# Four products of the first unit in half contractions, two of them in the k^T v banks, and a new set of ranks for the front

## Chip, cores and metric

The kernel runs on one core of one Trainium2 chip. The metric is the device time of one execution in microseconds (us), from runs of the whole kernel; lower is better.

## What is computed

Linear attention with 8 batches of 8 heads, 576 positions and 64 channels a head, then a mixture of 8 experts over the 4608 tokens, weighted by a Sinkhorn-balanced routing matrix:

```python
phi = lambda x: np.where(x > 0, x, np.exp(x) - 1.0) + 1.0
q_p, k_p = phi(q), phi(k)
kv  = einsum('bhsd,bhse->bhde', k_p, v);  z = k_p.sum(axis=2)
x   = einsum('bhsd,bhde->bhse', q_p, kv) / (einsum('bhsd,bhd->bhs', q_p, z)[..., None] + 1e-06)
# x becomes (4608, 512): tokens by 8 heads x 64
P = np.exp(logits - logits.max())            # logits = x @ w_gate, (4608, 8)
for _ in range(8):
    P /= P.sum(1, keepdims=True) + 1e-09
    P /= P.sum(0, keepdims=True) + 1e-09
    P *= N / E
out = sum over e of P[:, e:e+1] * (np.maximum(x @ w1[e], 0) @ w2[e])   # w1: 512x1024, w2: 1024x512
```

## The kernel before

**A planner writes the order.** The kernel doesn't issue its work in the order of the source. Every step is added to a plan (`_Plan.add`) with the engine or engines it may run on, a cost, the steps it depends on, the buffers that it takes, and a priority. `_Plan.run` then plays the plan: whenever an engine is free, the step that can start first is taken, among those ready the one with the lowest priority number, and its instructions are emitted. Each engine then runs its instructions in exactly that order on the chip. The costs, the added latencies (`lat`) and the release times (`after`) are numbers in the source; they decide the order, and nothing else. At the end of the source a string of ranks gives some 240 steps another priority, and in part a fixed engine: `92:3.7509:dve` sets step 92's priority to 3.7509 and puts it on DVE. Steps are counted in the order in which they are added.

**The attention front.** `att(b, g)` is one of 16 attention steps, counted n = 2b + g; each handles four heads of one batch. Its loads `kin`, `qin`, `vin` (L253, 576 KB each) have two buffers per name, so the load of step n waits until step n - 2 has used its own. SP issues them, except those of n = 2 and 3, which POOL issues between the loads of w1 and w2 of expert 0 (L207, two halves each, converted to 16 bits on the way). Then come, by name of the tile:

- `ek`, `eq`: exp on ACT (L266), then the minimum with 1 on DVE (L275)
- `tk`, `tq`: the feature map. Either ACT adds 1 (L272) and DVE takes the maximum (L278), or DVE does both in two pieces (L281)
- `vv`: v as 16 bit (L221 on ACT, L223 on DVE)
- `kv_ps`: k^T v on PE (L309), 18 matmuls, in the PSUM banks `ye2` and `ye3`; its copies `kvz`, four small ones, on ACT or DVE
- `qt_ps`: nine transposes of tq (L335), copied to `qpT` in two pieces
- `den_ps` (L350), `rden` with its reciprocal (L356, L358), `num_ps` (L374), `xn` in three pieces (L379, DVE)
- `xt_ps`: transposes of xn (L390), copied to the shared `xT` (L221, L223), which holds x transposed for the whole kernel

`logits` (L408) and the routing iterations follow when the batches they need are there. Ahead of the first real matmul, and between the early ones, PE runs 47 warm-up matmuls, `yw` (L481), of lowest priority.

**Expert 0.** `unit_plain(0, g)` for nine groups g of 512 tokens does the two plain layers: `layer1` makes eight products `hq` of 128 x 512 (L546, four matmuls each, one for each quarter c of the contraction over 512 channels), each followed by a ReLU on ACT (`h`, L550); then the second layer makes four products `ye` of eight matmuls (L736), cut in two halves of four: the first needs only the first half of w2, the second the other. The results are copied to `acc` (ACT L221 or DVE L223). The planner puts these products between the attention steps; unit 0 is g = 0.

**PSUM.** There are eight banks: `ye0` to `ye3`, two of `hq` (pool `hqp`), two of `att` (pool `aps`, which qt, den, num, xt and logits share). A product of unit 0 needs a bank of its own until its ReLU has read it.

**Half contractions.** The quarters c = 0, 1 of `xT` come from attention step n = 0, the quarters c = 2, 3 from n = 1. In unit 0 the first two products are cut in two jobs, the first of which needs only n = 0:

```python
jobs = [(f, 0, NDT) for f in range(NFT)]
if g == 0:
    jobs = [(f, c, c + 2) for c in (0, 2) for f in range(2)] + jobs[2:]
```

**Experts 1 to 7** (`block7`, L640, and `unit`, L843) use products with combined operands that save one of eight. They need `x_blocks`, which stores combinations of `xT` in `xd` by SP, to be loaded again as `xs` (L598). The order of their PE work is written out by hand in `order`, and the ranks of this change don't reach it.

Of the kernel before, what the change touches and what calls it, by code (L numbers as in the profile page):

```python
# [10 lines left out]
FP32 = mybir.dt.float32  # L11
# [111 lines left out]
def kernel(  # L123
# [17 lines left out]
    P = 128  # L141
# [4 lines left out]
    NFT = F // P  # L146
# [4 lines left out]
    S_ = _Plan()  # L151
# [5 lines left out]
    yps = ctx.enter_context(tc.tile_pool(name="yps", bufs=1, space=PSUM))  # L157
    hqp = ctx.enter_context(tc.tile_pool(name="hqp", bufs=2, space=PSUM))
# [26 lines left out]
    p_att, p_hq, p_h = S_.pool(2), S_.pool(2), S_.pool(2)  # L185
# [4 lines left out]
    p_ye = [S_.pool(1) for _ in range(4)]  # L190
# [41 lines left out]
    def fadd(*a, **kw):  # L232
        t = add(*a, **kw)
        front_ids.append(t)
        return t

    def att(b, g):
        n = 2 * b + g
        pr = n - 100.0
# [7 lines left out]
        gin, tin, gt, tph = {}, {}, {}, {}  # L247
        for nm, ten in (("k", k), ("q", q), ("v", v)):
            gr = gin[nm] = S_.grp(p_in[nm])

            def fn(_, gr=gr, nm=nm, ten=ten):
                gr["tile"] = fp.tile([P, 2, NJ, D], FP32, tag=nm + "in", name=nm + "in", bufs=2)
                (nc.gpsimd if n in (2, 3) else nc.sync).dma_start(  # L253
                    out=gr["tile"].rearrange("p r j d -> p r (j d)"),
                    in_=AP(tensor=ten.tensor, offset=(b * H + 4 * g) * S * D, ap=src))
            ti = fadd(("pool", 1.0) if n in (2, 3) else ("sp", 0.45), fn, acq=[gr], prio=pr,
                      deps=[w_last[0] if n in (2, 3, 4) else None, in_prev[0]])
            in_prev[0] = ti
            tin[nm] = fadd(("dma", 1.55), lambda _: None, deps=[ti], use=[gr], prio=pr, lat=2.6)
        for nm in "kq":  # L260
            ge = S_.grp(p_e)
            gt[nm] = S_.grp(p_t[nm])
# [30 lines left out]
        def f_v(e):  # L293
            copy(e, gvv["tile"][:, :, :, 0:D], gin["v"]["tile"])
        tvv.append(fadd(("act", 1.17) if n < 2 else ("dve", 0.75), f_v, deps=[ta, tin["v"]],
                        use=[gvv, gin["v"]], prio=pr))
# [32 lines left out]
        for j0, j1 in ((0, 5), (5, NJ)):  # L329
# [8 lines left out]
            def f_qc(e, j0=j0, j1=j1, gp=gp):  # L338
# [3 lines left out]
                           use=[gp, gq], prio=pr))  # L342
# [147 lines left out]
    for i in range(2):  # L490
        nc.vector.memset(vv_t[i][:, :, :, D], 1.0)
        nc.vector.memset(kvz_t[i], 0.0)
    att(0, 0)
    att(0, 1)
    w_t = {0: load_w1(0, prio=-290.0, parts=2, deps=[gates[0]])}
    for b in range(1, B):
        att(b, 0)
        att(b, 1)
        if b == 1:
            w_t[0] += load_w2(0, prio=-96.5, parts=2, deps=[in_prev[0]])  # L500
        if b % 2 == 1:
            logits(b // 2)
# [22 lines left out]
    def layer1(e, g):  # L525
        gw1, tw1, gw2, tw2 = w_t[e]
        bs = range(512 * g // S, (512 * g + 511) // S + 1)
        xd_ = [xt_done[(b, c)] for b in bs for c in range(NDT)]
        th = []
        gh = S_.grp(p_h)  # L530

        def f_ha(_):
            gh["tile"] = hpool.tile([P, NFT, 512], FP16, tag="h", name="h")
        tha = add(("none", 0.0), f_ha, deps=[prev_hq[0]], acq=[gh], prio=g - 400.0)
        ghqs = [S_.grp(p_hq) for f in range(NFT)]
        jobs = [(f, 0, NDT) for f in range(NFT)]
        if g == 0:
            jobs = [(f, c, c + 2) for c in (0, 2) for f in range(2)] + jobs[2:]
        for f, c0, c1 in jobs:
            ghq = ghqs[f]  # L540

            def f_hq(_, f=f, ghq=ghq, c0=c0, c1=c1):
                if c0 == 0:
                    ghq["tile"] = hqp.tile([P, 512], FP32, tag="hq", name="hq")
                for c in range(c0, c1):
                    nc.tensor.matmul(ghq["tile"], lhsT=gw1["tile"][:, c, ts(f, P)], rhs=xT[:, c, ds(512 * g, 512)],  # L546
                                     start=(c == 0), stop=(c == NDT - 1))

            def f_rl(_, f=f, ghq=ghq):
                nc.scalar.activation(out=gh["tile"][:, f, :], in_=ghq["tile"], func=AF.Relu)  # L550
            t1 = add(("pe", 0.2175 * (c1 - c0)), f_hq, deps=[tw1[f // 4], prev_hq[0]] + xd_[0:c1 if g == 0 else None],
                     acq=[ghq] if c0 == 0 else [], use=[gw1] + ([ghq] if c0 > 0 else []),
                     prio=g + 0.1 * f + 0.35)
            prev_hq[0] = t1
            x_users.append(t1)
            if c1 < NDT:
                continue
            th.append(add(("act", 0.6), f_rl, deps=[t1, tha], use=[ghq, gh], prio=g - 400.0))
        return gh, [th, th]
# [369 lines left out]
    for tt in (3, 2, 1, 0):  # L929
# [2 lines left out]
            chain.append(pe_id[f"z{tt}{half}"])  # L932

    ranks = """
        43:-88.9997 46:-94.9994:act 55:-94.9991:dve 56:-94.9985:dve 66:4.15 68:-94.9985 71:-89.0006
        74:-392.9979:dve 85:-89.0003:dve 92:3.7509:dve 96:-97.9985 99:-94.9991:dve 107:-392.9967
        110:-95.0006:act 133:-94.9991 139:-95 146:4.1497 152:-88.9994 153:-94.9994:dve 154:-94.9997
        166:-95.0003:act 172:-398.0018:dve 173:4.1497:dve 174:-97.9988:dve 199:-398.0021 200:-94.9988
        209:-88.9991 216:-94.9973 226:-94.9991 235:-94.9997 246:-90.9976:dve 248:-94.9997 255:-95.0003:act
        256:-90.9973:act 257:-397.9985:act 261:-94.9997 263:-95.0003 265:-397.9994 267:-392.9982 269:-398  # L940
        284:-95.0003:dve 286:-95 288:-398.0024 290:-95.0009 294:-392.9976:act 296:-95.0042:dve 298:-95.0003
        299:-98:dve 300:-94.9991 305:-95.0006 307:-95.0003 309:-397.9988 310:-392.9997 311:-393.0006 321:-95
        323:-95.0006 324:-88.9994 326:-95 328:-88.9997 331:-90.9982 334:-392.9985:act 338:-94.9991 340:-94.9997
        343:-97.9997 349:-89.9994 350:-95.0015:dve 353:8.3497 362:-97.9997:act 366:-88.9985 370:-95.0006
        376:-94.9994 377:-90.9985:dve 378:-88.9988 379:-90.0012:act 383:-95.0006 385:-90.9985 387:-88.9991
        392:-90.0018:dve 403:-94.9979:act 406:-95.0009 408:-88.9988 411:-85.0009:dve 414:-89.0009 416:-88.9991
        418:-88.9994 421:-90.0018 423:-395.0012 427:-95.0018 429:-90.0018 444:-88.9997 446:-88.9985
        447:-97.9991:act 448:-90.9997:act 454:-85.0009 459:-89.0012 461:-90.9988 463:-90.9982 467:-95.0018
        476:-90.0012:dve 482:-90.0015 486:-94.9973:act 487:-90.0009:act 488:-89:act 490:-89.9997
        491:-95.0015:act 492:-95.0009 493:-90.0012:dve 494:-395 499:-85.0015 501:-90.9985 505:-99.003  # L950
        516:-95.0012:act 526:-89.0003:act 532:-395.0015 533:-94.9988 534:-90.9985 535:-395.0021 540:-90.9979
        543:-394.9994 545:-395.0006 554:-90.0012 563:-395.0012 565:-395.0012:dve 569:-90.9982 571:-85.0015
        573:-89.9997 576:-96.0006 578:-96 580:-90.9979 585:8.3482:dve 593:-90.9976:act 595:-85.0006
        601:-395.0024 607:-89.0021 609:-90.9985 616:3.75 618:-95.0042 630:-89.0003 640:-88.9988 646:-96.0009
        647:-395.0015:dve 648:-395.0012 650:-395.0009 653:-395.0018 655:-97.9994 659:3.7515 666:8.3485
        671:-90.9985 678:8.7491 684:8.6479 717:-99.003 723:-95.0009 725:-94.9994:dve 731:-398.0021:act
        733:3.7509 735:-98 742:-94.9994 744:-94.9991 749:-95.0003 754:-94.9994 756:-94.9991 759:-398.0003
        762:-95.0003 763:-95.0003 764:-97.9997 768:-90.0012:act 769:8.3491 774:8.6485 776:8.6488 791:-94.9976
        793:-90.0009 796:-90.0015 797:-90.9985 799:-89.0006 800:4.1515 801:-88.9991 803:-95.0006 804:-95.0003
        806:-89.9988 809:-90.0012:act 816:3.7512 818:-395.0006 824:-90.9988 826:-90.0018 830:-395 836:-90.0012  # L960
        838:-395.0009 839:-90.9985 840:-89.0009 844:-395.0018 845:-89.0006 850:-94.9982:act 854:-94.9979:act
        856:-395.0006 865:-88.9994 866:-90.0009 867:-90.9979 868:-88.9997 875:-395.0024 897:8.3494 898:3.75
        906:-85.0009 910:8.6509 916:-89 918:3.7494 920:-85.0012 924:3.7509 926:-395.0033 928:3.7497 929:-90.9994
        931:8.6512 938:-96.0015 947:1.7518 957:-395.0015 959:-96.0027 961:-96.0006 964:8.3488 969:8.3494
        979:3.7518 988:-90.9988 990:-90 992:8.3491 998:-395.0021 1000:3.7512 1006:3.7479 1009:8.7488 1010:8.7482
        1016:3.7512:act 1017:8.6518 1020:8.7503 1031:8.7494 1039:-85.0012 1041:-94.9997 1043:-90.9994
        1049:3.7518 1051:-95.0012 1052:8.6491 1060:8.3479 1061:8.6482
    """
    for w in ranks.split():
        n, p, *en = w.split(":")  # L970
# [35 lines left out]
```

## Time and profile before

| | us |
|---|---|
| median of 6 runs | 977.54 |
| the six runs | 975.72, 975.76, 975.84, 979.25, 979.57, 980.36 |
| profiled execution | 975.4 |
| its span | 973.6 |

| engine | busy us | share of the span |
|---|---|---|
| PE | 963.9 | 99% |
| DVE | 767.6 | 79% |
| ACT | 569.1 | 58% |
| POOL | 111.7 | 11% |

The span is the time from the first to the last instruction in the trace; the profiled execution's own time is 1.8 us longer. The share of PE counts a matmul as busy until its modelled end. The shares of DVE and ACT are means over stages that differ: the attention front takes the first 138 us, in which ACT is busy over 90% of most slices from 40 to 120 us. The granted TensorE clock is full throughout.

Where the loads of the start land, by issue and landing time (us): k, q, v of n = 0 at 5.1, 6.5, 8.1; of n = 1 at 9.6, 11.0, 12.5; w1's halves, issued at 8.2 and 9.0, at 15.2 and 17.75; k, q, v of n = 2 at 19.3, 21.2, 22.7; of n = 3 at 24.1, 25.6, 27.0; w2's halves, issued at 17.8 and 18.6, at 30.6 and 36.3; k, q, v of n = 4, issued by SP at 24.7, 26.5, 27.2, at 31.7, 35.1, 36.9.

### The profile page before, as it was taken

What the parts mean: (1) busy time and instruction counts of PE and PEld (TensorE: products, weight loads), DVE (VectorE), ACT (ScalarE), POOL (GpSimd) and SP (SyncE); (2) the same over time, 40 slices, a digit from 0 to 9 for tenths busy, and PEclk for the clock granted to TensorE, in tenths of its full rate; (3) what the DMA queues carried; (4) which work ended last, traced back from release to release, by engine and by line L of the source; (5) the groups of instructions that cost most, each with busy time, mean ns of one, the idle gap of its engine ahead of it and who ended that gap; (6) DMA issues with size and microseconds to landing.
All of it is one profiled execution on the core that took longest, in us unless ns stands there. A gap on an engine that the chain in (4) does not pass through costs nothing.

```text
span 973.6 us, 21442 instructions
## 1 busy us (share of the span) xinstructions
PE 963.9 (99%) x8737; PEld 794.0 (82%) x8737; DVE 767.6 (79%) x1563; ACT 569.1 (58%) x1049; POOL 111.7 (11%) x158
## 2 busy tenths in 40 slices
PE   8999999999999999999999999999999999999998
PEld 4556564588888888888888888888888888888886
DVE  6899778987777778777777777777777887777775
ACT  6899945555555555555555555555555555555553
POOL 3000000111111111111111111111111111111110
PEclk9999999999999999999999999999999999999999
DMA  9987925562227222272226222272226322236664
GB/s 317 283 271 241 231 78 189 168 147 77 76 77 157 84 76 77 80 160 75 75 73 133 92 73 73 73 161 77 74 76 139 101 77 77 77 100 166 161 161 109
DMA packets 47188, 121.99 MB, mean 125 GB/s; under 512 B 4208, under 2 KB 18288, under 8 KB 47088
## 3 DMA queue, kind: packets, MB, share of 16 engines
q1 hardware_dynamic: 32208, 99.76, 31.0%
q0 software_dynamic: 14480, 20.33, 11.7%
q8 instruction: 68, 1.11, 0.5%
q10 hardware_dynamic: 400, 0.52, 0.2%
q14 instruction: 32, 0.26, 0.1%
HBM read 119.69 MB, written 17.69 MB: 141 GB/s over the span
## 4 chain that ended last, share of the span: by engine, by line
PE 92%; ACT 3%; DMA 3%; DVE 1%; issue 1%; POOL 0%; ACTq 0%; DVEq 0%; POOLq 0%
PE ye L843 33%; PE hq L640 23%; PE att L640 11%; PE ye L736 6%; PE Zye L640 6%; PE Zye L843 6%; PE hq L546 4%; DMA w<-in_moe_w_dram 2%; PE yw L481 1%; DMA kin<-in_k_dram 1%; PE xt_ps L390 1%; ACT eq L266 1%; ACT h L550 1%; PE kv_ps L309 1%; PE num_ps L374 0%
## 5 line engine op out<-in xcount | busy, mean ns | idle before, releaser
L857 DVE SCALAR_TENSOR_TENSOR acc<-ye,P_sb,acc 128x256 f32<-128x256 f32 x620 | 264.7, 476 | 95.7 <-PE ye L843 78.7
L640 PEld LDWEIGHTS <-W 128*128 128x128 f16 x2016 | 197.1, 98 | 24.0 <-issue 0.2
L843 PEld LDWEIGHTS <-S 128*128 128x128 f16 x1984 | 194.2, 98 | 22.4
L843 PE MATMUL ye<-T,S 128*128 128x256 f16 x1488 | 192.8, 273 | 0.0
L666 ACT ACTIVATE h<-hq 128x512 f16<-128x512 f32 x126 | 76.3, 606 | 160.1 <-PE hq L640 160.1
L640 PEld LDWEIGHTS <-w 128*128 128x128 f16 x1512 | 147.5, 98 | 23.1 <-issue 0.8
L867 POOL TENSOR_TENSOR acc<-acc,st 128x256 f32<-128x256 f32 x124 | 87.6, 727 | 625.5 <-ACT st L864 620.6
L843 PEld LDWEIGHTS <-h 128*128 128x128 f16 x1488 | 145.6, 98 | 16.8
L640 PE MATMUL hq<-xs,W 128*128 128x256 f16 x1008 | 151.2, 273 | 0.0
L640 PE MATMUL att<-xs,W 128*128 128x256 f16 x1008 | 151.2, 272 | 0.0
L640 PE MATMUL hq<-xs,w 128*128 128x256 f16 x1008 | 140.7, 272 | 0.4 <-DVE h L669 0.3
L816 DVE TENSOR_TENSOR S<-h 128x1024 f16<-128x1024 f16 x124 | 85.2, 687 | 58.2 <-ACT h L666 58.2
L864 ACT ACTIVATE st<-Zye,P_sb 128x256 f32<-128x256 f32 x124 | 52.1, 471 | 78.3 <-PE Zye L843 78.3
L656 ACT COPY s<-hq 128x512 f32<-128x512 f32 x126 | 75.0, 595 | 36.7 <-PE hq L640 36.7
L669 DVE CUSTOM_DVE_ANT_0 h<-att,s 128x512 f16<-128x512 f32 x126 | 86.6, 687 | 11.5 <-ACT s L656 11.0
L663 ACT ACTIVATE h<-Zye 128x512 f16<-128x512 f32 x126 | 75.3, 597 | 34.8 <-PE Zye L640 34.8
L669 DVE CUSTOM_DVE_ANT_0 h<-hq,s 128x512 f16<-128x512 f32 x126 | 86.4, 686 | 0.1
L652 ACT COPY Zye<-hq 128x512 f32<-128x512 f32 x126 | 73.2, 581 | 17.5 <-PE hq L640 17.5
L736 PE MATMUL ye<-w,h 128*128 128x512 f16 x312 | 75.6, 379 | 0.5 <-ACT acc L221 0.3
L640 PE MATMUL Zye<-xs,w 128*128 128x256 f16 x504 | 75.6, 273 | 0.0
L660 ACT COPY s<-att 128x512 f32<-128x512 f32 x126 | 74.5, 591 | 0.0
L546 PE MATMUL hq<-xT,w 128*128 128x512 f16 x288 | 70.3, 379 | 0.9 <-ACT h L550 0.7
(95 smaller groups left out, 960.4 us busy)
## 6 DMA issues: line engine op xcount, KB each, us to landing
xs<-xd SPq DMA_DIRECT2D x63, 896.0 KB, 4.6
w<-in_moe_w_dram POOLq DMA_DIRECT2D x14, 1024.0 KB, 11.3
out_dram<-acc SPq DMA_DIRECT2D x67, 128.0 KB, 2.4
kin<-in_k_dram SPq DMA_DIRECT2D x14, 576.0 KB, 5.5
qin<-in_q_dram SPq DMA_DIRECT2D x14, 576.0 KB, 5.5
vin<-in_v_dram SPq DMA_DIRECT2D x14, 576.0 KB, 6.2
xd<-xst SPq DMA_DIRECT2D x9, 512.0 KB, 2.9
xd<-xT SPq DMA_DIRECT2D x9, 256.0 KB, 3.2
```

The source lines that it names most:

```text
L546: nc.tensor.matmul(ghq["tile"], lhsT=gw1["tile"][:, c, ts(f, P)], rhs=xT[:, c, ds(512 * g, 512)], start=(c == 0), stop=(c == NDT - 1))
L640: nc.tensor.matmul(dst[:, p, :], lhsT=lhs(p, c), rhs=rhs(c), start=(first and p == 0 and c == 0), stop=(c == 1), skip_group_check=True)
L656: nc.scalar.copy(out=gs2["tile"], in_=gX["tile"])
L660: nc.scalar.copy(out=gs5["tile"], in_=gR["tile"])
L663: nc.scalar.activation(out=hd(0, 0), in_=Zt[1], func=AF.Relu)
L666: nc.scalar.activation(out=hd(1, 0), in_=gX["tile"], func=AF.Relu)
L669: nc.vector._custom_dve(TENSOR_ADD_SAT, out=dst, in0=ps, in1=sb, s0=3.0e38, s1=0.0)
L736: nc.tensor.matmul(gy[tt]["tile"], lhsT=gh["tile"][:, f, ds(P * tt, P)], rhs=gw2["tile"][:, f, :], start=(f == 0), stop=(f == NFT - 1))
L816: nc.vector.tensor_tensor(out=Sx[:, i], in0=a0, in1=a1, op=op)
L843: nc.tensor.matmul(bank(g_)[:, s, :], lhsT=lhs(s, kk), rhs=rhs(kk), start=(new and s == 0 and kk == 0), stop=(kk == 3), skip_group_check=True)
L857: nc.vector.scalar_tensor_tensor(out=dst(), in0=bank(g_)[:, s, :], scalar=P_sb[:, gg, e:e + 1], in1=dst(), op0=ALU.mult, op1=ALU.add)
L867: nc.gpsimd.tensor_tensor(out=dst(), in0=dst(), in1=gst["tile"], op=ALU.add)
```

## The change

Three things change in the source. In the planner the loads of the attention get a latency of 2.95 instead of 2.6; that is a number the planner sorts by. In unit 0, four products instead of two are cut in half contractions, and the products f = 2 and 3 take their PSUM banks from `ye2` and `ye3`, the banks of k^T v, instead of waiting for the two `hq` banks. And the string of ranks is replaced as a whole, which also fixes other engines for some steps; since unit 0 now has twelve jobs instead of ten, the steps added after it have other numbers.

```diff
-            tin[nm] = fadd(("dma", 1.55), lambda _: None, deps=[ti], use=[gr], prio=pr, lat=2.6)
+            tin[nm] = fadd(("dma", 1.55), lambda _: None, deps=[ti], use=[gr], prio=pr, lat=2.95)
...
-        ghqs = [S_.grp(p_hq) for f in range(NFT)]
+        ghqs = [S_.grp(p_ye[f] if g == 0 and f in (2, 3) else p_hq) for f in range(NFT)]
         jobs = [(f, 0, NDT) for f in range(NFT)]
         if g == 0:
-            jobs = [(f, c, c + 2) for c in (0, 2) for f in range(2)] + jobs[2:]
+            jobs = [(f, c, c + 2) for c in (0, 2) for f in range(4)] + jobs[4:]
...
                 if c0 == 0:
-                    ghq["tile"] = hqp.tile([P, 512], FP32, tag="hq", name="hq")
+                    own = g == 0 and f in (2, 3)
+                    ghq["tile"] = (yps if own else hqp).tile([P, 512], FP32, tag=f"ye{f}" if own else "hq", name="hq")
...
     ranks = """
-        43:-88.9997 46:-94.9994:act 55:-94.9991:dve 56:-94.9985:dve 66:4.15 68:-94.9985 71:-89.0006
...
+        19:-94.9997 20:-94.9988 27:-98.9994 34:900.0003 42:-98.9976 53:-87.9991:act 54:-290:act 58:0.9509
...
```

What the program then holds, engine by engine, in the order of its instructions up to about the first output products:

- PE: 30 warm-ups, kv and qt of n = 0; qt, kv of n = 1 (kv and qt before); the four xt; then the eight half products c = 0, 1 and c = 2, 3 of f = 0 to 3, f4, f5; qt and kv of n = 2; f6, f7; den, two num, kv of n = 3, the other num; the first half of `ye0`; ten xt of n = 2; the first half of `ye1`; qt of n = 3; then the second half of `ye1`. Before, f4 to f7 stand among the same attention steps, and the second half of `ye0` comes after five xt of n = 2 and den of n = 3.
- DVE: after the last xn of n = 1, directly ek and tk of n = 2, where before two copies of xT stand between. ACT takes three of the four first xT copies. tk of n = 0 is made by ACT and DVE, tq by DVE alone (the other way round before).
- POOL: w1's first half, k, q, v of n = 2, w1's second half, k, q, v of n = 3, w2's halves. Before, w1's second half stands directly behind its first.
- ACT: after qpT of n = 3, acc of the first `ye1`, then ek of n = 4. Before, ek and the addition for tk of n = 4 come ahead of that acc.
- SP: the same loads in the same order; after the front, the blocks of `xd` are stored in another order, group 0's among the first two.

## The prediction

> **What bounds the kernel now.** I read the table by slices first. PE is busy in every slice, and from 110 us to the end it never waits:
>
> ```profile
> PE   8999999999999999999999999999999999999998
> ...
> 110.00:140.00 30.00, 30.00 (x401) 19.76 (x401) 20.48 (x50) 18.27 (x38) 1.07 (x2) 1.00 0.28 53
> 140.00:188.00 48.00, 48.00 (x235) 23.04 (x233) 43.13 (x123) 24.37 (x42) 0.40 (x1) 1.00 0.60 211
> ```
>
> (Window, sum, then busy us of PE, PEld, DVE, ACT, POOL.) The PE work is the same in both kernels, so the time can only move by the idle and warm-up time of PE before 110 us. The windows of that part:
>
> ```profile
> 24.00:36.30 12.30, 11.45 (x121) 6.58 (x121) 10.40 (x24) 8.98 (x18) 0.00 (x0) 1.00 1.15 296
> 36.40:46.00 9.60, 9.60 (x98) 5.66 (x97) 8.05 (x16) 9.20 (x12) 0.00 (x0) 1.00 0.72 238
> 46.00:66.00 20.00, 19.02 (x206) 11.21 (x206) 18.66 (x40) 19.55 (x37) 0.00 (x0) 1.00 0.87 290
> 66.00:86.00 20.00, 19.94 (x206) 12.06 (x204) 18.52 (x39) 19.45 (x33) 0.00 (x0) 1.00 0.83 294
> 86.00:110.00 24.00, 23.68 (x247) 14.25 (x244) 20.12 (x47) 22.21 (x36) 0.93 (x2) 1.00 0.81 247
> ```
>
> After 36.4 us they show 0.98 + 0.06 + 0.32 = 1.4 us idle. A 512-column matmul is drawn 0.38 us long but issues every 0.216, so each stall hides 0.16 more; counted from starts, some nine stalls make 2.8 us. ACT (19.55 of 20) and DVE (18.66 of 20) are nearly full: they feed the attention, and PE waits for them. The DMA share is above 1 up to 36 us. The chain of waits shows what that does:
>
> ```profile
> 17.85 0.74 POOL w L207
> 18.58 17.75 DMA w<-in_moe_w_dram
> 36.37 1.02 PE ye L736 x4
> ```
>
> The second half of w2, issued at 18.58, lands at 36.33, and the first `ye` product that needs it starts at 36.37. This is a fixed post that PE can't pass early. Up to it, the PE timeline reads (start, length, what, and in brackets idle before it):
>
> ```profile
> 21.11 0.59 PE L546 MATMUL hq<-xT,w 128*128 128x512 f16 x2
> 21.54 0.72 PE L390 MATMUL xt_ps<-ident,xn 128*128 128x128 f16 x10
> 22.10 0.38 PE L481 MATMUL yw<-warm 128*128 128x512 f16 x1
> 22.53 1.46 PE L546 MATMUL hq<-xT,w 128*128 128x512 f16 x6
> 24.26 1.89 PE L546 MATMUL hq<-xT,w 128*128 128x512 f16 x8 [0.27 <-ACT h L550]
> 26.47 0.68 PE L335 MATMUL qt_ps<-ident,tq 128*128 128x128 f16 x9 [0.33 <-DVE tq L281]
> ...
> 33.31 1.03 PE L736 MATMUL ye<-w,h 128*128 128x512 f16 x4
> ```
>
> [...] a kvz copy ready at 11.1 us ran on DVE at 13.40, behind an ek and a tk. [...] a half of w1, undisturbed, took 2.55 us (15.2 to 17.75), the second half of w2, with SP's loads of n = 4 beside it, 5.7 us (30.6 to 36.3).
>
> **The change, part by part.** n counts the 16 attention steps, f the eight products of unit 0.
>
> *Two more banks and split products.* No instruction is added: 47 warm-ups, 288 hq, 264 ye, the same attention work ahead of the first `block7` in both programs. In the new order all eight first halves stand behind the four transposes of n = 0, 1, so they cover only the copies of the last two of them. Four halves before, 1.73 us, cover less than the wait; eight, 3.46 us in all with their second halves, cover it. The gap of 0.27 for bank f0 also goes, because f2 and f3 have banks of their own.
>
> *New ranks up to the post.* I follow the new order on DVE from tq of n = 1, which ends near 15.7 (15.88 before): rden with reciprocal 0.5, two xn of 512 1.3, two kvz 0.4, xn of 256 0.4, rden with reciprocal 0.5, xT 0.4, three xn 1.6. That is 20.8; before, the last xn ended at 21.45. Two xt 0.55 lead to the first hq at 21.4 (21.11 before). Sixteen dense matmuls end at 24.9; before, four whole products ended at 25.98. f4 and f5 follow at once, to 26.6, where tq of n = 2 (25.5) is ready: the stall of 0.33 goes. kv and qt (1.15) and f6, f7 (1.73) end at 29.5, den 0.3, a wait for vv of n = 3 (30.4), kv 0.65, num 0.5: the first `ye` starts at 31.6 instead of 33.31. **PE is 1.7 us ahead.** Then `ye` 0.86, 0.5 of waiting for the last xn of n = 2 (32.95), xt 0.56, `ye` 0.86, qt 0.5: PE stands at the product with w2's second half at 34.9. What it has done by then is what the old order had done at 36.37, but for five xt in place of ten den (0.28 against 0.27). So the lead is worth nothing unless that half lands earlier; it is turned into a wait of 1.4 us.
>
> *Later landings and POOL's queue.* The 2.95 is a number of the planner alone. It moves w1's second half behind k, q, v of n = 2. By the landings of before (15.2, then 1.5 us for each load and 2.55 for the half) it lands at 22.3; f4 wants it at 24.9, so 2.6 us cover it. Bytes ahead of w2 on that queue stay the same. But k of n = 4 on SP waits for the kin buffer that tk of n = 2 frees:
>
> ```profile
> 23.16 1.43 DVE L281 SCALAR_TENSOR_TENSOR tk<-kin,ek 128x576 f16<-128x576 f32 x2
> 24.66 0.37 SPq L253 DMA_DIRECT2D kin<-in_k_dram  x1
> ```
>
> In the new order DVE goes from the last xn (20.8) straight to ek and tk (1.85 us), so this load starts at 22.7, 1.9 earlier[...]. SP's loads got 4.3 us of service (5.7 and 3.75 for w2's halves, against 2.55 each) in the 10.3 up to 36.3, a share of 0.42. With 1.9 us more of sharing, w2 lands 1.9 x 0.42 / 0.58 = 1.4 later at most, not at all later at least. I take **1.0 us, at 37.3**.
>
> *From the post to 63 us.* Up to the fourth `ye` half of unit 1 both orders hold 23.3 us of PE work (10 ye, 8 hq, 3 kv and so on by the times above). Before had done it, and two more ye halves (1.73), by 63.3 us: 63.3 - 1.7 - 36.4 = 25.2 us, stalls of 1.9. ACT's new order has acc of the first `ye1` ahead of ek of n = 4, so ACT sits from 35.6 to 38.2 with 1.05 us operations queued behind it, where before it did ek and tk at 36.81 and 37.88. xn of n = 3, kv of n = 4 and its qt then come late: stalls of 0.35, 0.1 and 0.5; later 0.45 at qt of n = 5 behind tq, 0.2 at an xt, 0.4 at ye behind the last relu, 0.3 in small ones: 2.3. Together 1.0 + 0.4, rounded to **+1.4 us**.
>
> *From 63 to 110 us.* Before has 1.3 us of stalls there. Up to the last xT copy the new program gives DVE 5 acc copies (0.69) and 4 kvz (0.22) more, 3 qpT (0.45) and one xT (0.45) fewer: +2.5 us; ACT about +0.7. PE has 12 ye fewer and 36 logits more in between, 1.7 us less to hide behind. This row has no counterpart in the trace: at best the stalls vanish (-1.3), at worst all of the 2.5 reaches PE. I take +0.1.
>
> *Past 110 us.* Nothing: PE has ready products (first `block7` at 188, its inputs never waited for), and the copies to `xd` of group 0 move forward on SP. If that cover went, a landing of `xs` (4.6 us) would show.
>
> Sum: +1.5 us on the profiled 975.4 us (span 973.6 and 1.8 around it), 976.9. That execution lies 2.1 under the median of 977.54, whose six runs fall into 975.7 to 975.8 and 979.3 to 980.4. On the median: **979.0**.
>
> **Rivals.** *Slower:* DVE's 2.5 us more lands on the attention chain between 63 and 115 us, where ACT is full already and can't take it back. With the 1.4 it gives +3.9, 981.4. It decides from 1.5 us of new stalls there. For it: DVE at 18.5 of 20; against it: 20.1 of 24 after 86. *Faster:* w2's half isn't late, or lands at 34.9 because the queue wastes less, and the new ranks remove the stalls after it: 1.5 - 1.0 - 1.4 - 1.3 - 0.4 = -2.6, 974.9. For it: the lead of 1.7 at the first `ye` is real; against it: the DMA share above 1. *The split does nothing:* the order could have been had by ranks alone, and the four banks cover no more than the 0.27 and 0.43 seen around 24 us; within 0.7 us of the forecast.
>
> **Numbers.** About 0.3% (2.9 us) is what a measurement can tell from no change. Likeliest case 0.48, with an own range of 976.6 to 980.4; slower rival 0.38; faster 0.14. Two levels of the runs, 3.7 us apart, widen both ends: 974.9 to 983.0.
>
> **What would show it.** Right: first `ye` near 31.6, a PE wait of 1.4 us or more ended by the DMA of w near 37, k of n = 4 issued near 22.7, ACT idle near 36 to 38. Wrong: the product with w2's second half starting before 36, or PE idle of less than 0.5 us from 37 to 110; on the slow side, windows 66 to 110 with over 2 us idle.

## The result, and the profile after

The changed kernel takes 981.97 us in the median of 34 runs (977.95 to 984.99), against 977.54 of 69 runs of the kernel before (974.94 to 983.99). The ratio compares the mean times (981.8 and 978.1) and is 1.0038, with a 95% interval of 1.0029 to 1.0047: about 3.7 us slower. The medians lie 4.4 us apart. The forecast was 979.0 (974.9 to 983.0). The profiled execution took 981.53 us, its span 979.7 (before: 975.4 and 973.6).

The slices and windows of the changed kernel, in the columns that the prediction explained:

```profile
PE   8899999999999999999999999999999999999998
...
36.40:46.00 9.60, 7.56 (x48) 3.85 (x45) 5.06 (x11) 4.88 (x6) 0.00 (x0) 0.82 0.44 144
46.00:66.00 20.00, 18.87 (x230) 11.81 (x229) 18.69 (x39) 19.29 (x33) 0.00 (x0) 1.00 0.87 292
66.00:86.00 20.00, 19.51 (x209) 11.32 (x207) 19.04 (x42) 19.79 (x32) 0.00 (x0) 1.00 0.66 225
86.00:110.00 24.00, 23.72 (x247) 14.61 (x246) 21.47 (x49) 22.25 (x37) 0.97 (x2) 1.00 0.88 289
110.00:140.00 30.00, 29.36 (x372) 19.07 (x371) 22.20 (x48) 17.47 (x35) 1.32 (x2) 1.00 0.42 89
```

Two rows stand out. In 36.4 to 46 us PE is busy 7.56 of 9.60 where it was busy all the time before, and the clock (the column after POOL) is 0.82. And 110 to 140 us, full before, now has 0.64 us idle, with DVE at 22.20 instead of 20.48. The PE timeline of the changed kernel shows the first:

```profile
22.79 5.35 PE L547 MATMUL hq<-xT,w 128*128 128x512 f16 x24 [1.53 <-DMA w<-in_moe_w_dram]
...
33.01 1.02 PE L737 MATMUL ye<-w,h 128*128 128x512 f16 x4
...
38.61 1.17 PE L737 MATMUL ye<-w,h 128*128 128x512 f16 x4 [2.04 <-DMA w<-in_moe_w_dram]
...
39.88 1.87 PE L737 MATMUL ye<-w,h 128*128 128x512 f16 x4
```

The 24 `hq` matmuls in one run are the new order at work: no warm-up and no gap between them. But they start behind a wait for w1, and the product with w2's second half starts at 38.61 behind 2.04 us of waiting; before it was 36.37. Four matmuls right after it take 1.87 us where 1.02 is usual. SP's queue shows what the prediction named as the reason for a late landing, k of n = 4, issued at 22.48 (before 24.66):

```profile
22.48 0.37 SPq L253 DMA_DIRECT2D kin<-in_k_dram  x1
```

One way of dividing the time will be used for every run below. **The post** is the start of the product with w2's second half. **The rest** is the span less the post. PE's work up to it is equal in both orders to within 0.01 us, by the prediction's count, so the rests of all these kernels can be compared. Before: post 36.37, rest 937.2. After: 38.61 and 941.1. The later post is 2.2 us of the 6.1 us between the two spans; the rest grew by 3.9.

### The profile page after: what moved, and what is told of

Its sections match the earlier page's. It is cut to its first block, busy times and chain, and to the rows that moved or that the text cites. A ratio compares the mean times of both kernels' runs of the same rounds, so it can differ in the third digit from the quotient of the medians.

```text
span 979.7 us, 21425 instructions
## 1 busy us (share of the span) xinstructions
PE 965.5 (99%) x8737; PEld 794.6 (81%) x8737; DVE 771.7 (79%) x1568; ACT 567.7 (58%) x1044; POOL 110.0 (11%) x158
## 4 chain that ended last, share of the span: by engine, by line
PE 88%; DVE 2%; ACT 0%; issue 0%; ACTq 0%
PE ye L844 33%; PE hq L641 23%; PE att L641 11%; PE Zye L641 6%; PE Zye L844 6%; PE ye L737 4%; PE hq L547 4%; DVE h L670 0%; PE xt_ps L390 0%; DVE xn L379 0%; DVE tq L281 0%; PE num_ps L374 0%; PE lg_ps L408 0%; PE qt_ps L335 0%; PE kv_ps L309 0%
```

## Experiments

Theory A is the prediction's: w2's second half lands late because SP loads k, q, v of n = 4 beside it. Rival B is the slower one: DVE's added work, spread over the attention steps later on. A third cause, the PE clock after a long wait, came from the profile after. The ratios below are to runs of the kernel before that were made beside each experiment; their medians are 978.15 (e1 to e4), 978.33 (e5 to e8) and 977.71 (e9).

**A correction of the prediction's account of w1.** The addresses of the loads in the program show that the new ranks issue the half of w1 with columns 512 to 1023 at 8.72 us and the half with columns 0 to 511, which f = 0 to 3 read, behind k, q, v of n = 2. The list of the engines' orders and the prediction had them the other way round. In e2 and e3 the edit issues both halves back to back in the later slot, near 12.5 us, not directly after 8.7.

**e1: n = 4 behind w2.** k, q, v of n = 4 go to POOL's queue, behind w2:

```diff
-                (nc.gpsimd if n in (2, 3) else nc.sync).dma_start(
+                (nc.gpsimd if n in (2, 3, 4) else nc.sync).dma_start(
```

> The changed kernel with one edit: POOL issues k, q, v of n = 4 behind w2's halves, instead of SP beside them; no order on PE, ACT or DVE moves. Theory A (the late second half of w2 is the main cost: a PE wait of 2.04 us, and the halved clock behind it, some 1.4 us): the half lands near 33 us instead of 38.4, PE doesn't wait for it, the clock stays full, and 3.5 us or more of the loss go: about 978.3, a ratio to before of 1.001 or less. Rival B (the attention rounds after 44 us with more work on DVE are the main cost): at most 2 us of the loss go, ratio 1.002 or more, and the windows 44 to 140 us stay as idle as in the changed kernel. Against both: k of n = 4 lands near 35.5 us instead of 30; ACT wants it at 38, so nothing should wait.

Measured: 978.61 us (22 runs), ratio to before 1.0006 (0.9997 to 1.0016). w2's second half lands at 32.2 instead of 38.6, and a low mean clock is left in 1 of 22 runs. Its PE timeline:

```profile
36.36 1.03 PE L737 MATMUL ye<-w,h 128*128 128x512 f16 x4
...
108.96 1.02 PE L547 MATMUL hq<-xT,w 128*128 128x512 f16 x4 [1.08 <-ACT h L551]
```

No bracket at the first line: the wait for w2 is gone, and with it about 3.1 us of the 3.7 (1.0038 to 1.0006), the share of the low clock included. Theory A holds for the wait: the loads beside w2 cause it. But the rest is 940.7, not 937.2, and the second line, a stall that before doesn't have, lies far behind w2.

**e2: both halves of w1 together.** In the changed kernel:

```diff
-            ti = add(("pool", 1.0), fn, use=[g], prio=prio, deps=[tal])
+            ti = add(("pool", 1.0), fn if nm != "w1" or parts == 1 else
+                (lambda _, fn=fn, i=i: i or [fn(_, j) for j in range(parts)]), use=[g], prio=prio, deps=[tal])
```

> The changed kernel with one edit: w1's second half is issued directly behind its first, as before the change; no order on PE, ACT or DVE moves. The first hq product waited 1.53 us until that half had landed (22.7 us), although it reads the first half alone. Theory A: the first hq starts near 21.3 us instead of 22.79, the first ye near 31.5 instead of 33.01, and all of it turns into a longer wait for w2's second half, which still lands near 38: time unchanged within 0.7 us, ratio 1.003 to 1.005, with the clock low for as long or longer. Rival: the lead is kept and 1.5 us are gained, ratio 1.0023. If the wait at the first hq had another cause, it starts at 22.8 as before.

Measured: 980.96 us (7 runs), 1.0046 (1.0029 to 1.0063). The first `hq` starts at 21.59 instead of 22.79, and the PE timeline ends that lead:

```profile
34.22 1.02 PE L737 MATMUL ye<-w,h 128*128 128x512 f16 x4 [2.27 <-DMA w<-in_moe_w_dram]
...
39.84 1.87 PE L737 MATMUL ye<-w,h 128*128 128x512 f16 x4 [2.67 <-DMA w<-in_moe_w_dram]
```

With SP's load of n = 4 in place, a lead ahead of w2 is worth nothing; both halves of w2 are waited for.

**e3: both edits together.**

> The changed kernel with both edits of the loads. Theory A: now the lead isn't stopped by w2, so the 1.5 us at the first hq count too: 1.0 to 1.5 us below the kernel with n = 4 behind w2 alone, about 977, ratio 0.9995. Rival B: ratio still 1.0015 or more. If it comes out under 0.997, the new ranks and the split are worth something by themselves once the loads are mended.

Measured: 977.15 us (14 runs), 0.9995 (0.9984 to 1.0007). The first `hq` starts at 21.04 without a wait, and the post is passed at 34.64 without one:

```profile
34.64 1.03 PE L737 MATMUL ye<-w,h 128*128 128x512 f16 x4
```

This is the lead of 1.7 us that the prediction worked out (34.9 against 36.37), now real. Yet the time is that of the kernel before: the rest is 940.0, so 2.8 us are given back behind the post.

**e4: the kernel before, with n = 4 behind w2** (the edit of e1).

> The kernel before with the one edit that POOL issues k, q, v of n = 4 behind w2's halves. Its PE comes to the product with w2's second half at 36.1 us and waits 0.29 us there. Theory A: 0.3 us in a run like the profiled one, and up to 2 us in those of its runs in which the loads are slower: ratio 0.998 to 1.000. Rival: k of n = 4, which ACT wants at 36.8 us here, comes later than that (near 35.5 at best), and the kernel gets slower: ratio 1.001 or more.

Measured: 975.06 us (13 runs), 0.9978 (0.9967 to 0.9989): the fastest kernel of this study, and faster than both. Its profiled execution (post 36.42, rest 936.9) is nearly that of the profile of before, so the gain of the median isn't seen in that trace; e9 to e11 come back to it. This kernel and e3 both have w2 in time, so the two compare the orders, the split included: 11 of the 13 runs of e4 are below the fastest of e3, and the medians lie 2.1 us apart. The new order is the slower one, though it passes the post 1.8 us earlier (34.64 against 36.42).

**e5: the wait filled.** The changed kernel with eight warm-up matmuls ahead of the product that waits, to keep PE busy:

```diff
+    fill8 = lambda: [nc.tensor.matmul(fw, lhsT=warm[:, 0:P], rhs=warm, start=True, stop=True)
+        for fw in [hqp.tile([P, 512], FP32, tag="hq", name="yfill")] * 8] and None
...
-                    for f in range(4 * half, 4 * half + 4):
+                    for f in (fill8() if (e, g, tt, half) == (0, 0, 1, 1) else None) or range(4 * half, 4 * half + 4):
```

> The changed kernel with eight more warm-up matmuls (128x512, result unused, 1.73 us at full clock) on PE directly ahead of the ye product that waits for w2's second half. In the changed kernel PE idles there from 36.5 to 38.6 us, and the granted clock is 0.68, 0.50, 0.50, 0.61 in the four us from 39 on. Theory A1 (the idle wait itself lowers the clock, and this costs about 1.4 us on top of the wait): the clock stays at 1.0 from 39 to 43 us, the wait is still ended by the DMA of w near 38, and the time falls by 1 to 1.5 us: ratio 1.0023 to 1.0028. Rival: the drop has another cause: clock low again, ratio 1.0038 or more.

First the windows of the changed kernel behind its wait (the clock is the last but two):

```profile
39.00:40.00 1.00, 1.00 (x14) 0.61 (x13) 0.00 (x0) 0.19 (x1) 0.00 (x0) 0.68 0.84 311
40.00:41.00 1.00, 1.00 (x4) 0.30 (x2) 0.46 (x2) 1.00 (x2) 0.00 (x0) 0.50 0.25 83
...
42.00:43.00 1.00, 1.00 (x8) 0.65 (x7) 1.00 (x3) 0.51 (x1) 0.00 (x0) 0.61 0.00 0
```

Measured with the fill: 980.43 us (22 runs), 1.0029 (1.0018 to 1.0040). In its profiled execution the clock is 1.00 in every window from 36 to 44 us:

```profile
40.00:41.00 1.00, 1.00 (x7) 0.44 (x5) 1.00 (x3) 1.00 (x2) 0.00 (x0) 1.00 0.34 127
```

The mean clock over a run, which the runs list, was 0.998 or less in 23 of 34 runs of the changed kernel and in 2 of 22 with the fill. So the low clock comes from PE's idling there. In the time the gain is at most small: the interval overlaps that of the changed kernel, and the fill takes 1.73 us itself.

**e6: the halves of w1 exchanged in place**, with the edit of e1:

```diff
-            ti = add(("pool", 1.0), fn, use=[g], prio=prio, deps=[tal])
+            ti = add(("pool", 1.0), fn if nm != "w1" or parts == 1 else
+                (lambda _, fn=fn, i=i: fn(_, 1 - i)), use=[g], prio=prio, deps=[tal])
```

> The changed kernel with two edits of loads: k, q, v of n = 4 behind w2 on POOL, and w1's halves exchanged in their two places on POOL's queue. The new ranks issue the second half of w1 (columns 512 to 1023) first and the first half behind k, q, v of n = 2, so the first hq product has to wait for it at 22.7 us. Theory A: the first hq starts near 21.2 us, and 1 to 1.5 us of the time of the kernel with n = 4 behind w2 alone (978.6) go: 977.2, ratio 0.999 to 1.000, as in the kernel with both halves together. If the halves didn't matter, it is at 1.0006 again.

Measured: 977.40 us (14 runs), 0.9985 (0.9969 to 1.0001). The first `hq` starts at 21.00 without a wait, the post is at 34.61; the rest is 941.1, with one long stall in the PE timeline:

```profile
107.63 1.02 PE L547 MATMUL hq<-xT,w 128*128 128x512 f16 x4 [1.44 <-ACT h L551]
```

**e7: e6 with the acc copies of g = 1 to 4 on ACT**, which takes the five copies that the new order gave DVE in the front off it again:

```diff
-                    copy(eng, acc[g][:, tt, :], gy[tt]["tile"])
+                    copy("act" if 1 <= g <= 4 else eng, acc[g][:, tt, :], gy[tt]["tile"])
```

> The kernel of e6_w1_swapped_n4 with the six acc copies that the new ranks gave DVE for g = 1 to 4 done by ACT, at the same places of the order (DVE 6 x 0.69 = 4.1 us less before 115 us, ACT 6 x 0.59 = 3.5 us more). Rival B in its own form (DVE's extra work between 63 and 115 us is what PE waits for there): 1 to 1.5 us faster than e6_w1_swapped_n4, stalls by DVE xn and tq after 63 us mostly gone. Against it: ACT is as full as DVE there, so it becomes the one waited for: no gain, or up to 1.5 us slower.

Measured: 977.05 us (22 runs), 0.9988 (0.9977 to 0.9999), not to be told from e6. DVE's busy time from 70 to 150 us fell from 66.3 to 65.1 (before 64.4, after 67.4). The PE timeline has waits for ACT, one of them for a moved copy:

```profile
61.48 1.02 PE L737 MATMUL ye<-w,h 128*128 128x512 f16 x4 [0.51 <-ACT acc L221]
```

Moving the copies alone doesn't cure it. The rest of this profile, 939.7, is shorter than e6's 941.1, but e3, without this edit, has 940.0: single profiles don't tell such a difference apart.

**e8: the split without the new ranks.** The edit of e1 and the change's bank edit in the kernel before, the old ranks carried over to the shifted step numbers:

```diff
-        t = S_.t[int(n)]
+        n = int(n)
+        for x in extra:
+            n += n >= x
+        t = S_.t[n]
```

> The kernel before with n = 4 behind w2 (ratio 0.9978), and of the change the split alone: four half-contraction products, two in the k^T v banks, with the ranks of before for all other steps. The split removes the waits of 0.27 and 0.2 us for an hq bank and lets four more halves fill: if it works as such, 0.5 to 0.8 us faster, ratio 0.9971. Rival: the planner writes another order around it that costs more: ratio 0.9985 or more. If it is the same within 0.3 us, the split is worth nothing by itself.

Measured: 998.96 us (4 runs), 1.0208 (1.0183 to 1.0232), far outside every case named. The planner wrote another order from some 26 us on: the last logits came at 173 us (before 138.5), the routing later still, and DVE did scalings of `acc` between 212 and 239 us, in the work of experts 1 to 7. The longest PE wait in its timeline:

```profile
239.46 1.86 PE L847 MATMUL ye<-w,S 128*128 128x256 f16 x8 [9.87 <-DVE acc L861]
```

That says nothing of the split: a set of ranks is tied to one list of steps. What the split alone is worth stays open.

**e9: the kernel before with four warm-up matmuls at the post.** e4 gained 2 us on the kernel before, and low mean clocks had stood beside the longer runs of before; e9 to e11 ask whether the kernel before has the wait for w2 as well, in some executions.

```diff
+    filled = []
+    fill8 = lambda: filled.append(1) or [nc.tensor.matmul(fw, lhsT=warm[:, 0:P], rhs=warm, start=True, stop=True)
+        for fw in [hqp.tile([P, 512], FP32, tag="hq", name="yfill")] * 4] and None
...
-                    for f in range(4 * half, 4 * half + 4):
+                    for f in (fill8() if half == 1 and not filled else None) or range(4 * half, 4 * half + 4):
```

> The kernel before with 4 warm-up matmuls (0.86 us at 0.216 each) ahead of the first product that needs w2's second half. In 43 of the 93 runs of the kernel before that stood beside the experiments so far, the mean clock was 0.998 or less, with a median near 979.5 against 976.8 in the others; with the loads of n = 4 behind w2 it was 1 of 13. Theory C: these are executions in which w2's second half lands 1 to 2 us late, PE idles for it near 36 to 39 us, and runs at half clock for some 3 us after. Then the fill takes the low clock from nearly all runs (at most 1 in 10 left), the levels come together near 977.3, and the ratio is 0.998 to 1.000. Rival D: the low clock has another cause or place. Then it stays in about half of the runs, and the 0.86 us is added on top: 1.0005 to 1.001.

Measured: 977.46 us (20 runs), 1.0003 (0.9992 to 1.0014). A mean clock of 0.998 or less is left in 2 of 20 runs; in the runs of before beside it, it was 6 of 23. The median is the one that theory C gave; the ratio lies just over its range, since this time before had few such runs. In the profiled execution, the PE timeline shows how late the old order's load can be:

```profile
40.02 1.02 PE L737 MATMUL ye<-w,h 128*128 128x512 f16 x4 [1.69 <-DMA w<-in_moe_w_dram]
```

Post 40.0, rest 937.7. POOL issued that half at 18.44, no later than in the profile of before (18.58), and the fill had ended 1.69 us ahead. So a post 3.6 us later than in the profile of before came from the landing alone.

**e10 and e11: the kernel before again, unchanged.**

> The kernel before, unchanged, for a second profile. With a mean clock of 0.998 or less (about one chance in two), theory C expects the product with w2's second half at 37.5 or later behind a PE wait of 1 us or more ended by the DMA of w, and a stretch of some 3 us at half clock straight after it; rival D expects the stretch elsewhere. With a mean clock of 0.999 or 1.0 it expects that product near 36.4, and nothing is told apart.

> As the second profile of the kernel before: a third one, since each has about one chance in two of showing the low clock. Theory C: low mean clock together with a PE wait of 1 us or more for w2's second half near 37 us. Rival D: low mean clock without it.

Measured: 975.45 us (post 36.43, rest 937.3, no wait) and 976.0 us, both with a mean clock of 1.0, so the case with the low clock wasn't caught. The third profile has a wait all the same, in the PE timeline:

```profile
36.82 1.02 PE L736 MATMUL ye<-w,h 128*128 128x512 f16 x4 [1.10 <-DMA w<-in_moe_w_dram]
```

So the kernel before does wait for w2 in some executions, and this one had run ahead by the 0.9 us that it started its first `hq` earlier (20.57, against 21.45 in e10). That its runs with a low clock are those with a longer wait is likely from e4 (1 low clock in 13 runs) and e9, but no trace shows it.

**e12: the changed kernel again, unchanged.**

> The changed kernel, unchanged, for a second profile. The late landing of w2's second half is fixed by the order, so the PE wait for it is expected again, 1.5 to 2.5 us ended near 38 to 39 us. The half clock after it is expected in 2 of 3 executions; if the mean clock is 1.0, the product after the wait runs at 0.216 us a matmul and the execution is near 980.0 instead of 982.5.

Measured: 978.65 us, span 976.9, mean clock 0.999. The PE timeline at the post:

```profile
37.15 1.02 PE L737 MATMUL ye<-w,h 128*128 128x512 f16 x4 [1.26 <-DMA w<-in_moe_w_dram]
```

The wait is shorter than expected, the clock stays full, and the time is below the 980.0 named. Post 37.15, rest 939.8.

## Why the prediction was right or wrong

| | old order: before, e4, e9, e10, e11 | new order: after, e1, e2, e3, e5, e6, e7, e12 |
|---|---|---|
| post, us | 36.4, 36.4, 40.0, 36.4, 36.8 | 38.6, 36.4, 39.8, 34.6, 37.5, 34.6, 34.7, 37.2 |
| rest, us | 937.2, 936.9, 937.7, 937.3, 937.4 | 941.1, 940.7, 942.1, 940.0, 939.3, 941.1, 939.7, 939.8 |

The rest is the same within 0.8 us wherever the order is the old one, and 1.6 us or more longer in every run of the new one, however early or late w2 lands. (After and e2 hold the low clock in it, about 1.5 us in after.)

**The range held the time, by the wrong case.** The forecast's own case was within 0.3% of before; the kernel is slower by 0.38%, the case that stood at 0.38. That this case's 981.4 lies so near the median of 981.97 is luck in part: it has no term for the clock, which most of the runs of the changed kernel pay.

**The post: right in kind, and in size in one execution of two.** k of n = 4 was expected at 22.7 and came at 22.48; a PE wait of 1.4 us ended by the DMA of w near 37.3 was expected: it was 1.26 at 37.15 in e12 and 2.04 at 38.61 in the first profile. The +1.0 measured +0.8 and +2.2. What the sum lacked is that this landing isn't one number: w2's second half landed at 35.9, 36.3, 36.8 and 40.0 us in the old order (e10, before, e11, e9) and at 37.1, 37.5 and 38.6 in the new one (e12, e5, after). That the loads of n = 4 beside it make it late is shown by e1 and e4, where it lands at 32.2 in both orders. That their start 2 us earlier makes it later still, the step that the +1.0 rests on, isn't shown: executions of one order differ by more.

**The walk up to the post: right but for one load.** The first `ye` was forecast at 31.6 and came at 33.01; with the wait for w1 taken away it is at 31.2 in e6. The step that failed is "it lands at 22.3; f4 wants it at 24.9": it was the other half, wanted at 21.4. In the first profile it cost 1.5 us of a lead that w2 would have stopped anyway (e2).

**The clock: not in the sum.** The prediction priced a PE wait at its length. In the first profile the four windows from 39 us show 0.68, 0.50, 0.50 and 0.61, together 3.4 us at half clock. Counted from the post, matmuls start some 1.5 us later there than in e12, at full clock. By the mean clocks this happens in 23 of 34 runs of the changed kernel (median 982.5, against 979.9 in the other 11) and, in three groups of runs, in 49 of 116 of the kernel before.

**From the post to 63 us: about right.** The extra of 0.4 us can be held against PE's time from start to start: what each interval between the starts of two instructions has over the time that the first takes when its kind runs without gaps. Summed from 40 to 70 us it is 2.4 to 2.8 us in before, e10 and e11, and 2.8 in e12, so the extra lies between nothing and the 0.4. The stalls named at the qt of n = 4 and n = 5 are in e12's trace (0.47 at 45.27, 0.62 at 50.30).

**From 63 us on: the step that failed.** It took +0.1 up to 110 us and nothing past that. From 70 to 150 us the same measure is -0.1, 0.1 and 0.0 us in before, e10 and e11, 0.5 in e9 and -0.6 in e4; it is 2.2 in after and in e12, and 1.6 to 3.0 in the other runs of the new order. So about +2 where +0.1 was taken; which time is taken as that without gaps moves the figure by some 0.3. The groups of PE from 44 to 150 us, first of before, then of after (busy and mean | idle before, and what ended it):

```profile
L335 PE MATMUL qt_ps<-ident,tq 128*128 128x128 f16 x108 | 9.5, 219 | 0.1
L350 PE MATMUL den_ps<-kvz,qpT 128*128 128x2 f16 x120 | 4.9, 166 | 0.4 <-ACT kvz L221 0.4
```

```profile
L335 PE MATMUL qt_ps<-ident,tq 128*128 128x128 f16 x108 | 9.6, 219 | 1.2 <-DVE tq L281 0.7 <-DVE tq L278 0.2 <-DVE xn L379 0.2
L350 PE MATMUL den_ps<-kvz,qpT 128*128 128x2 f16 x120 | 5.0, 166 | 0.7 <-DVE xn L379 0.3 <-ACT qpT L221 0.2 <-DVE qpT L223 0.2
```

The waits at qt and den changed hands: ACT's kvz before, mostly DVE's tq, xn and qpT now. DVE's busy time from 70 to 150 us is 67.4 and 67.7 us (after, e12) against 64.4. This points to the slower rival, "DVE's 2.5 us more lands on the attention chain", whose price of 2.5 was near. The prediction's evidence against it, DVE at "20.1 of 24 after 86", misled: a share of 0.84 over a window doesn't say that its operations come in time for PE. The windows to watch were named as 66 to 110 us; they show 0.8 us idle, under the 2 named, and a good part of the idle time lies past them, where the prediction said "Nothing". That the amount of DVE's work is the cause isn't shown: in e7 the five added copies (3.4 us) are back on ACT and the median falls by only 0.35 us, but then PE waits for ACT, which is as full (19.45 of 20 us from 66 to 86 in e7). What costs is the new order after the post (e4 against e3); which single step in it would be enough to change is open.

**The sum, redone.** Without the low clock (e12 against before, e10 and e11): spans 976.9 against 973.6 to 974.2, so 2.7 to 3.3 us. Of it 0.3 to 0.8 is the post and 2.4 to 2.6 the rest. The first profile adds 1.5 us at the post and about 1.5 for the clock. "The split does nothing" wasn't settled (e8). The faster rival needed both its conditions: e3 and e6 fulfil the first, w2 in time, and end 0.0005 to 0.0015 below before, intervals reaching to no change, because the second, no new stalls behind it, fails.

## What to carry to other kernels

When a product waits for a load, look at what the other queues do in that time: putting the next step's loads behind it in the same queue was worth about 3.1 us here and, in the kernel before, made the best version, 0.9978. A lead won ahead of such a load is worth nothing until the load comes earlier (e2: 1.2 us at the first `hq`, and 1.0046), and what an order shifts behind it has to be priced over the whole stretch that follows, to the last step that the order touches. Split two kernels at one event that both pass with the same work done, and compare the times on either side: one table then told the load from the order in thirteen profiles.

## What the hardware showed that was not expected

**A PE wait of 2 us can cost more than its length.** In the changed kernel's first profile PE had waited 2.04 us up to 38.61, and the clock was 0.50 from 39.36 to 42.77. The four `ye` matmuls started at 39.88 took 1.87 us; the same four in e12, behind a wait of 1.26 us, took 1.02. The length of a wait alone doesn't tell. e2 has two: the four matmuls behind the one of 2.27 us, ended at 34.22, took 1.02 us, and the next four, at 35.63, 1.03; those behind the one of 2.67 us, ended at 39.84, took 1.87. The mean clock was 1.0 in the executions with the waits of 1.10 (e11) and 1.69 us (e9), and 0.999 in the one with 1.26 (e12). What besides the length decides isn't shown, and so neither is why 23 of the 34 runs of the changed kernel have a low clock and 11 don't.

**One load's landing varied by some 4 us between executions of one order** (35.9 in e10 and 40.0 in e9), with no later issue of that load in the second (18.92 and 18.44). No single profile of such a kernel gives the price of that wait.
